# Reordering the first batch of a fused cosine-attention and feed-forward kernel: key tiles ahead of values, transposes ahead of sums

## The chip, the cores and the metric

One core of a Trainium2 chip runs the whole kernel. The metric is device time in microseconds (us): the median over several executions. Beside it stands one profiled execution, from which every duration of an instruction is read. The engines are called by the profile's names: PE (matmul), PEld (its weight loads), DVE (vector), ACT (activation), POOL (general purpose) and SP (issues transfers). Each engine works through its own list of instructions in order and waits at an instruction whose inputs or buffers are not ready.

## The reference

Attention with normalised queries and keys over 8 batches of 12 heads, 448 positions of 64 numbers each, then a feed-forward layer on the 3584 tokens:

```python
def _attn_ref(q, k, v, tau):
    q_n = q / (np.linalg.norm(q, axis=-1, keepdims=True) + 1e-06)
    k_n = k / (np.linalg.norm(k, axis=-1, keepdims=True) + 1e-06)
    scores = np.matmul(q_n, k_n.transpose(0, 1, 3, 2)) / tau
    scores = scores - np.max(scores, axis=-1, keepdims=True)
    attn = np.exp(scores)
    attn = attn / (np.sum(attn, axis=-1, keepdims=True) + 1e-09)
    return np.matmul(attn, v)

def _moe_ref(x, w_in, w_out):          # x: 3584 x 768, w_in: 768 x 2048
    h = x @ w_in
    g = np.maximum(0.01 * h, h)
    return g @ w_out
```

## The kernel before

The unit of attention is a pair of heads (a slot `s`). Batch 0 has six pairs, `s` = 0 to 5; two pairs make a quad `j`. The order of all instructions is written out by hand, and each engine's list is the order of the calls in the Python text.

A pair goes through these steps. `squares(s)` multiplies q and k with themselves on POOL (for pair 0 and half of pair 1 on ACT and DVE). `sums(s, parts)` adds the 64 squares of each row on DVE; part 0 is q, part 1 is k. `roots(s)` makes norms on ACT with two instructions, `Ln` with the tile `tiny` (1e-18) as its bias (L244) and `Exp` with scale 0.5 (L245). `normalise(s)` adds 1e-6, takes reciprocals and writes `qn` (L253, L254, L270, all DVE). `transposes(s)` turns `qn` with seven PE instructions (L284) and copies them from PSUM to `qkT` on DVE (L325). `scores(s, kis)` computes key tiles on PE (L346): tile `ki` is 128 keys against 448 queries for both heads, and an `Exp` on ACT follows it (L355, 128x896). Tile 3 holds the last 64 keys of two pairs, so a quad has seven tiles. `totals(j)` sums the exponentials with 16 PE instructions (L366) and inverts them on ACT with `Ln` and `Exp` (L377, L378). `products(j, e)` are 16 PE instructions each that multiply with the values (also L366), and `scale(j, e)` on DVE (L397) divides them into `xT`, the input of the feed-forward part.

`first(c, m, kts)` are feed-forward products with `w_in` (L494), one PE instruction for each `kt`; six `kt` make an output. `second` multiplies with `w_out` (L527) and copies to `osb` (L538). Output columns `kt` 0 and 1 come from quad 0, 2 and 3 from quad 1, 4 and 5 from quad 2.

PSUM has eight banks. In batch 0 key tiles take turns on two pairs of banks, so the third tile cannot start before the exponential of the first has been read; single banks are the other four. `fill(count)` puts matmuls on PE whose results nobody reads (L603). `WARM` = 22 of them run at the start, before pair 0's data is there. `hold(x)` makes POOL wait for a tile of DVE, so that POOL's squares and transfers keep in step.

The loop over the pairs of batch 0 is this, cut to its PE and ACT steps:

```python
scores(s, (0,))
if s == 1: roots(2)
if j is not None and not even: products(j, 1)
scores(s, (1,)); fill(2)
...            # sums, normalise(s + 1), scale, hold, squares, loads
scores(s, (2,))
if last: first(0, 0..1, (0, 2))
elif not even or s == 0: fill(2)
if n and not even: roots(n)
if not even: scores(s, (3,))
if j is not None and even: totals(j)
if not last: transposes(s + 1)
if j is not None and even: products(j, 0)
if last: first(0, 0..1, (1,))
elif not even or s == 0: fill(2)
if n and even: roots(n)
```

Here `n` = s + 2 for s = 1 to 3, `j` = s // 2 - 1 from s = 2, `even` and `last` speak of `s`. After the loop come `totals(2)`, both `products(2, e)`, then the second batch's pairs (s = 6 to 11) between feed-forward groups, the third part written out with `settle` and `attend(j)` (totals, two products, two scales). From slot 12 on (`OLD`) other functions transpose and multiply in a steady stream (L306, L417, L442) with feed-forward groups between them, to the end.

## Time and profile before

| What | us |
|---|---|
| median of 3 runs | 420.97 (419.59 to 421.17) |
| profiled execution, its own time | 419.61 |
| its span, first to last instruction | 417.8 |
| PE busy | 409.2 (98%) |
| ACT busy | 253.7 (61%) |
| DVE busy | 219.8 (53%) |
| POOL busy | 114.8 (27%) |

The profiled execution's time is its span and 1.8 us around it, and it lies 1.36 us under the median, near the fastest of the runs. PE's busy time counts the `fill` matmuls, 49 in all, as work. Busy shares are averages over stages: batch 0's attention is the first 34 us of the span, and the steady stream begins near 83 us.

### The profile page before, as it was taken

What the parts mean: (1) busy time and instruction counts of PE and PEld (TensorE: products, weight loads), DVE (VectorE), ACT (ScalarE), POOL (GpSimd) and SP (SyncE); (2) the same over time, 40 slices, a digit from 0 to 9 for tenths busy, and PEclk for the clock granted to TensorE, in tenths of its full rate; (3) what the DMA queues carried; (4) which work ended last, traced back from release to release, by engine and by line L of the source; (5) the groups of instructions that cost most, each with busy time, mean ns of one, the idle gap of its engine ahead of it and who ended that gap; (6) DMA issues with size and microseconds to landing.
All of it is one profiled execution on the core that took longest, in us unless ns stands there. A gap on an engine that the chain in (4) does not pass through costs nothing.

```text
span 417.8 us, 11304 instructions
## 1 busy us (share of the span) xinstructions
PE 409.2 (98%) x4793; PEld 212.1 (51%) x4793; DVE 219.8 (53%) x385; ACT 253.7 (61%) x430; POOL 114.8 (27%) x150
## 2 busy tenths in 40 slices
PE   8899999999999999999999999999999999999996
PEld 3334554544455555544455555554445555654563
DVE  6877776866678565765484864464621301210021
ACT  4897877388757786667865688547774464014300
POOL 4877361433234132412331423122210000000000
PEclk9999999999999999999999999999999999999999
DMA  7999998684387941893285681742442100010022
GB/s 187 239 226 213 233 223 172 149 231 115 63 220 191 208 109 33 205 236 91 54 186 154 143 238 48 172 127 83 89 90 77 41 38 3 38 77 0 2 75 75
DMA packets 41810, 53.82 MB, mean 129 GB/s; under 512 B 12448, under 2 KB 32160, under 8 KB 41760
## 3 DMA queue, kind: packets, MB, share of 16 engines
q1 hardware_dynamic: 25584, 40.88, 35.2%
q0 software_dynamic: 15488, 11.80, 19.6%
q8 instruction: 37, 0.61, 0.6%
q10 hardware_dynamic: 688, 0.43, 0.4%
q14 instruction: 13, 0.11, 0.1%
HBM read 45.61 MB, written 11.01 MB: 136 GB/s over the span
## 4 chain that ended last, share of the span: by engine, by line
PE 96%; DVE 2%; ACT 2%; issue 0%; DVEq 0%
PE ps L527 36%; PE ps L494 35%; PE ps L442 9%; PE ps L417 7%; PE ps L366 3%; PE ps L603 3%; PE ps L346 2%; PE ps L284 1%; ACT pe L355 1%; DVE qkT L325 0%; DVE qn L270 0%; DVE ss L231 0%; DVE osb L538 0%; ACT ss L244 0%; ACT norms L245 0%
## 5 line engine op out<-in xcount | busy, mean ns | idle before, releaser
L527 PE MATMUL ps<-w_out_sb,hT 128*128 128x384 bf16 x896 | 151.3, 326 | 0.5 <-DVE xT L397 0.5
L494 PE MATMUL ps<-xT,w_in_sb 128*128 128x384 bf16 (+1 forms) x768 | 151.1, 353 | 0.0
L423 ACT ACTIVATE pe<-ps 128x896 bf16<-128x896 f32 x126 | 108.9, 916 | 44.7 <-PE ps L417 44.7
L527 PEld LDWEIGHTS <-hT 128*128 128x128 bf16 x896 | 85.5, 98 | 65.3 <-issue 10.8
L494 PEld LDWEIGHTS <-w_in_sb 128*128 128x128 bf16 x768 | 72.7, 98 | 74.1 <-issue 9.7
L505 ACT ACTIVATE hT<-ps 128x384 bf16<-128x384 f32 (+1 forms) x128 | 67.3, 553 | 54.7 <-PE ps L494 54.2
L538 DVE COPY osb<-ps 128x384 f32<-128x384 f32 (+1 forms) x56 | 30.9, 551 | 101.3 <-PE ps L527 101.2
L216 POOL TENSOR_TENSOR sq<-qk_h 128x896 f32<-128x896 f32 x36 | 60.4, 1679 | 3.8 <-DMA qk_h<-in_k_dram 3.8
L612 POOL CAST seen<-qn 128x1 f32<-128x1 bf16 x46 | 8.4, 183 | 184.6 <-DVE qn L260 167.8
L260 DVE TENSOR_TENSOR qn<-qk_h,r 128x896 bf16<-128x896 f32 x36 | 42.4, 1179 | 1.2
L355 ACT ACTIVATE pe<-ps 128x896 bf16<-128x896 f32 x42 | 36.0, 919 | 2.9 <-PE ps L346 2.8
L231 DVE TENSOR_REDUCE ss<-sq 128x14 f32<-128x896 f32 x36 | 37.4, 1038 | 0.0
L417 PE MATMUL ps<-qkT 64*32 64x448 bf16 x1008 | 36.5, 353 | 0.0
L253 DVE TENSOR_REDUCE r<-norms 128x14 f32<-128x28 f32 x48 | 8.6, 179 | 51.6 <-ACT norms L245 51.4
L244 ACT ACTIVATE ss<-ss,tiny 128x14 f32<-128x14 f32 x48 | 14.7, 307 | 26.6 <-DVE ss L231 25.7
L467 DVE TENSOR_TENSOR xT<-ps,rb 128x448 bf16<-128x448 f32 x32 | 18.4, 617 | 22.3 <-PE ps L442 21.2
L306 DVE STREAM_TRANSPOSE tt<-qn 128x448 f32<-128x448 f32 x36 | 29.5, 821 | 0.9
L442 PE MATMUL ps<-pe,vq 64*32 64x448 bf16 x1008 | 27.0, 349 | 0.0
L417 PEld LDWEIGHTS <-qkT 64*32 64x32 bf16 x1008 | 13.1, 91 | 19.3 <-issue 14.1
L442 PEld LDWEIGHTS <-vq 64*32 64x32 bf16 x1008 | 14.5, 93 | 8.0 <-issue 0.3
L603 PE MATMUL ps<-pe 128*128 128x512 bf16 x49 | 15.5, 443 | 1.6 <-DVE pe L586 1.6
L346 PE MATMUL ps<-qkT 64*64 64x448 bf16 (+1 forms) x132 | 12.8, 360 | 2.5 <-ACT pe L355 1.6
(55 smaller groups left out, 220.9 us busy)
## 6 DMA issues: line engine op xcount, KB each, us to landing
qk_h<-in_q_dram SPq DMA_DIRECT2D x36, 224.0 KB, 4.4
qk_h<-in_k_dram SPq DMA_DIRECT2D x36, 224.0 KB, 4.4
out_dram<-osb SPq DMA_DIRECT2D x20, 384.0 KB, 3.3
qkT<-tt SPq DMA_DIRECT2D x72, 56.0 KB, 3.1
qkT<-tt SPq DMA_DIRECT2D x36, 112.0 KB, 3.4
vq<-in_v_dram POOLq DMA_DIRECT2D x16, 224.0 KB, 5.0
w_in_sb<-in_moe_w_in_dram POOLq DMA_DIRECT2D x4, 768.0 KB, 11.0
w_out_sb<-in_moe_w_out_dram POOLq DMA_DIRECT2D x2, 1536.0 KB, 21.6
```

Of the source, the lines that this page charges most:

```text
L216: gp.tensor_tensor(sq, raw[s], raw[s], op=ALU.mult)
L231: nc.vector.tensor_reduce(ss[s], sqs[s].rearrange("p (t d) -> p t d", d=D), axis=AX.X, op=ALU.add)
L260: nc.vector.tensor_tensor(qn[s].rearrange("p m d e -> p m e d"), raw[s].rearrange(f"p ({t[1:-1]} d) -> p m e d", e=n, d=D), r.rearrange(f" ...
L306: nc.vector.transpose(out=to.rearrange(("p g (c m) -> p m g c", "p g (m c) -> p m g c")[which], m=7), in_=qn[s].bitcast(F32).rearrange("p ...
L355: nc.scalar.activation(out=dst, in_=sc[:, :, :S], func=AF.Exp, scale=inv_tau)
L417: nc.tensor.matmul(out=sc[32 * strip : 32 * strip + 32, a, :S], lhsT=x[rows, c0 : c0 + 32], rhs=x[rows, 0:S], start=True, stop=True,)
L423: nc.scalar.activation(out=pq[u, i], in_=sc[:, :, :S], func=AF.Exp, scale=inv_tau)
L442: nc.tensor.matmul(out=po[32 * strip : 32 * strip + 32, w, :S], lhsT=weights, rhs=pq[us[x if two else 0], i][rows, a, :], start=(i == 0), ...
L494: nc.tensor.matmul(out=pm[:, :n], lhsT=w_in_sb[:, kt, m * 128 : (m + 1) * 128], rhs=xT[c // 2][:, kt, c0 : c0 + n], start=(done + i == 0), ...
L505: nc.scalar.activation(out=hT[c][:, m, :n], in_=pm[:, :n], func=AF.Prelu, alpha=0.01)
L527: nc.tensor.matmul(out=po2[:, :HALF], lhsT=hT[c][:, m, ts * 128 : (ts + 1) * 128], rhs=w_out_sb[:, m, half * HALF : (half + 1) * HALF], st ...
L538: nc.vector.tensor_copy(out=o[:, half * HALF : half * HALF + cut], in_=po2[:, :cut])
```

## The change

Three things are edited. First, the loop over batch 0's pairs: for s = 3 and s = 5 key tile 1 stands in front of `products(j, 1)`; for s = 1 `roots(3)` moves behind key tile 3; for s = 3 `transposes(4)` moves in front of key tile 3; for s = 4 `transposes(5)` moves in front of `totals(1)` and key tile 0 of pair 5 in front of `products(1, 0)`; for s = 5 the `fill(2)` goes, and the two products `first(0, m, (3,))`, which stood behind `products(2, e)`, join those in front of `totals(2)`.

Second, the 1e-18: the squares of a row are kept in 65 columns, the last set once to 1e-18, so that the sum on DVE adds it and `Ln` has no bias tile. The three tiles of squares, `r` and `seen` become fixed tiles instead of tiles of a pool.

Third, two smaller moves: the first transfer on SP is the 64-row rest of q of pair 0 and no longer its main part, with the two squares and sums of that pair swapped to match; and `roots(s + 6)` (slot 12) stands behind `attend(3)` and not in front of it.

```diff
-            x[:, 0:512].rearrange("p (h t d) -> p h t d", h=2, d=D),
-            x[:, 512:896].rearrange("p (h t d) -> p h t d", h=2, d=D),
+            x[:, 0 : 8 * w].rearrange("p (h t d) -> p h t d", h=2, d=w),
+            x[:, 8 * w : 14 * w].rearrange("p (h t d) -> p h t d", h=2, d=w),
...
-        sq = sqp.tile([128, 14 * D], F32, name="sq")
+        sq = sqt[s % 3]
         if s >= OLD:
             sqs[s] = sq
-            gp.tensor_tensor(sq, raw[s], raw[s], op=ALU.mult)
+            x = raw[s].rearrange("p (t d) -> p t d", d=D)
+            gp.tensor_tensor(sq[:, :, :D], x, x, op=ALU.mult)
...
-                ss[s], sqs[s].rearrange("p (t d) -> p t d", d=D), axis=AX.X, op=ALU.add
+                ss[s], sqs[s], axis=AX.X, op=ALU.add
...
-        nc.scalar.activation(ss[s], ss[s], func=AF.Ln, bias=tiny)
+        nc.scalar.activation(ss[s], ss[s], func=AF.Ln)
...
+    load_rem((0,), (nc.sync, None))
     load_main(0, (nc.sync, nc.scalar))
-    load_rem((0,), (nc.sync, nc.scalar))
+    load_rem((0,), (None, nc.scalar))
...
-    tiny = cpool.tile([128, 1], F32, name="tiny")
-    nc.vector.memset(tiny, 1e-18)
+    sqt = []
+    for i in range(3):
+        sqt.append(cpool.tile([128, 14, D + 1], F32, name=f"sq{i}"))
+        nc.vector.memset(sqt[i][:, :, D], 1e-18)
+    r = cpool.tile([128, 14], F32, name="r")
+    seen = cpool.tile([128, 1], F32, name="seen")
...
-    for t in (slice(0, 3), slice(3, 4)):
+    for t in (slice(3, 4), slice(0, 3)):
...
-        scores(s, (0,))
+        if not last:
+            scores(s, (0,))
         if s == 1:
             roots(2)
+        scores(s, (1,))
         if j is not None and not even:
             products(j, 1)
-        scores(s, (1,))
-        fill(2)
+        if not last:
+            fill(2)
...
         if last:
             for m in range(2):
                 first(0, m, (0, 2))
-        elif not even or s == 0:
+            scores(s, (3,))
+            for kt in (1, 3):
+                for m in range(2):
+                    first(0, m, (kt,))
+        elif not even:
             fill(2)
-        if n and not even:
-            roots(n)
-        if not even:
+            if s == 3:
+                roots(n)
+                transposes(s + 1)
             scores(s, (3,))
-        if j is not None and even:
+            if s == 1:
+                roots(n)
+                transposes(s + 1)
+            fill(2)
+        elif s == 0:
+            fill(2)
+            transposes(1)
+            sums(2)
+            fill(2)
+        else:
+            if s == NPAIR - 2:
+                transposes(s + 1)
             totals(j)
...
+            if s == NPAIR - 2:
+                scores(s + 1, (0,))
+            else:
+                transposes(s + 1)
             products(j, 0)
-        if last:
-            for m in range(2):
-                first(0, m, (1,))
-        elif not even or s == 0:
-            fill(2)
-        if n and even:
-            roots(n)
+            if n:
+                roots(n)
...
-    for m in range(2):
-        first(0, m, (3,))
     for m in range(2, 4):
         first(0, m, range(KT - 2))
...
-    roots(s + 6)
     transposes(s + 5)
     attend(NQ)
+    roots(s + 6)
```

More of the change, by code (lines that the diff above doesn't have):

```diff
@@ L51 @@
     vbp = ctx.enter_context(tc.tile_pool(name="vb", bufs=3))
-    sqp = ctx.enter_context(tc.tile_pool(name="sq", bufs=3))
     smp = ctx.enter_context(tc.tile_pool(name="small", bufs=3))
@@ L118, with halves @@
     OLD = 2 * NEWQ
-    def halves(x):
+    def halves(x, w=D):
         return (
-            x[:, 0:512].rearrange("p (h t d) -> p h t d", h=2, d=D),
-            x[:, 512:896].rearrange("p (h t d) -> p h t d", h=2, d=D),
+            x[:, 0 : 8 * w].rearrange("p (h t d) -> p h t d", h=2, d=w),
+            x[:, 8 * w : 14 * w].rearrange("p (h t d) -> p h t d", h=2, d=w),
         )
@@ L131, in load_rem @@
         for i, (x, eng) in enumerate(zip((q, k), engs)):
+            if eng is None:
+                continue
             eng.dma_start(
@@ L212, in squares @@
             return
-        sq = sqp.tile([128, 14 * D], F32, name="sq")
+        sq = sqt[s % 3]
         if s >= OLD:
             sqs[s] = sq
-            gp.tensor_tensor(sq, raw[s], raw[s], op=ALU.mult)
+            x = raw[s].rearrange("p (t d) -> p t d", d=D)
+            gp.tensor_tensor(sq[:, :, :D], x, x, op=ALU.mult)
             return
-        sqs[s] = halves(sq)
+        sqs[s] = halves(sq.rearrange("p t d -> p (t d)"), D + 1)
         for x, y, eng in zip(raw[s], sqs[s], engs):
             if eng is nc.scalar:
-                nc.scalar.activation(y, x, func=AF.Square)
+                nc.scalar.activation(y[..., :D], x, func=AF.Square)
             else:
-                eng.tensor_tensor(y, x, x, op=ALU.mult)
+                eng.tensor_tensor(y[..., :D], x, x, op=ALU.mult)
     def sums(s, parts=(0, 1)):
@@ L251, in normalise @@
             return
-        r = smp.tile([128, 14], F32, name="r")
         nc.vector.tensor_reduce(r, norms[s % 3], axis=AX.X, op=ALU.add)
@@ L610, in hold @@
     def hold(x):
-        seen = smp.tile([128, 1], F32, name="seen")
         gp.tensor_copy(out=seen, in_=x)
-    sqs[0] = halves(sqp.tile([128, 14 * D], F32, name="sq"))
+    sqs[0] = halves(sqt[0].rearrange("p t d -> p (t d)"), D + 1)
     ss[0] = smp.tile([128, 14], F32, name="ss")
-    nc.vector.tensor_tensor(sqs[0][1], raw[0][1], raw[0][1], op=ALU.mult)
+    nc.vector.tensor_tensor(sqs[0][1][..., :D], raw[0][1], raw[0][1], op=ALU.mult)
     sums(0, (1,))
-    for t in (slice(0, 3), slice(3, 4)):
-        nc.scalar.activation(sqs[0][0][:, :, t], raw[0][0][:, :, t], func=AF.Square)
+    for t in (slice(3, 4), slice(0, 3)):
+        nc.scalar.activation(sqs[0][0][:, :, t, :D], raw[0][0][:, :, t], func=AF.Square)
         nc.vector.tensor_reduce(
@@ L696 @@
                 first(0, m, (0, 2))
-        elif not even or s == 0:
+            scores(s, (3,))
[3 more added lines that the diff above has]
+        elif not even:
             fill(2)
-        if n and not even:
-            roots(n)
-        if not even:
+            if s == 3:
+                roots(n)
+                transposes(s + 1)
             scores(s, (3,))
-        if j is not None and even:
-            totals(j)
-        if not last:
-            transposes(s + 1)
-        if s == 0:
-            sums(2)
-        if j is not None and even:
-            products(j, 0)
-        if last:
-            for m in range(2):
-                first(0, m, (1,))
-        elif not even or s == 0:
-            fill(2)
-        if n and even:
-            roots(n)
+            if s == 1:
[10 more added lines that the diff above has]
+                transposes(s + 1)
+            totals(j)
+            if s == NPAIR - 2:
+                scores(s + 1, (0,))
+            else:
+                transposes(s + 1)
+            products(j, 0)
+            if n:
+                roots(n)
         if j is not None and not even and not last:
```

## The prediction

> **What bounds the kernel now.** I read the page's engine rows first, then PE's waits, then PE and ACT in order of time for the first 66 us, then the chain around the one late wait.

> ```profile
> PE 409.2 (98%) x4793; PEld 212.1 (51%) x4793; DVE 219.8 (53%) x385; ACT 253.7 (61%) x430; POOL 114.8 (27%) x150
> PEclk9999999999999999999999999999999999999999
> ```

> PE is busy for all but 8.6 of 417.8 us, at a full clock. But its busy time holds 49 `fill` matmuls, so where it really could be shorter shows only in its waits:

> ```profile
> PE ps L346 <- ACT pe L355: 1.6, 5, 0.4
> PE ps L603 <- DVE pe L586: 1.6, 1, 1.6
> PE ps L346 <- DVE qkT L325: 0.9, 3, 0.3
> PE ps L527 <- DVE xT L397: 0.5, 1, 0.5
> ```

> The columns are total, times and longest. Apart from the start (1.6 us until the first `fill` has data) there are 3.0 us of waits, and each lies before 64 us: eight at key tiles of batch 0 (L346), one at a feed-forward group (L527). From 64 us on PE waits for nothing, so whatever is won or lost before that is carried to the end unchanged. The windows query says the same of the stretch 9.03 to 34.25: ACT is busy 21.98 of its 25.22 us, the highest share anywhere, and PE runs 28 fill matmuls there. That stretch is paced by ACT and its dependences; behind it PE sets the time. The two kinds of wait in order of time, PE first, then ACT:

> ```profile
> 17.95 0.36 PE L346 MATMUL ps<-qkT 64*128 64x448 bf16 x2 [0.29 <-DVE qkT L325]
> 18.74 0.36 PE L346 MATMUL ps<-qkT 64*128 64x448 bf16 x2 [0.42 <-ACT pe L355]
> ...
> 63.67 2.60 PE L527 MATMUL ps<-w_out_sb,hT 128*128 128x384 bf16 x15 [0.46 <-DVE xT L397]
> ```

> ```profile
> 17.33 0.31 ACT L244 ACTIVATE ss<-ss,tiny 128x14 f32<-128x14 f32 x1 [0.57 <-DVE ss L237]
> ...
> 30.86 0.92 ACT L355 ACTIVATE pe<-ps 128x896 bf16<-128x896 f32 x1 [0.33 <-PE ps L346]
> 32.02 1.75 ACT L355 ACTIVATE pe<-ps 128x896 bf16<-128x896 f32 x2 [0.25 <-PE ps L346]
> ```

> At 17.33 ACT stands in `roots(3)` waiting for a sum, with a finished key tile behind it; at 30.86 and 32.02 it waits for key tiles that PE has put behind products.

> **The change, part by part.**

> *Start, +0.1.* Three memsets of squares columns replace the one of `tiny` ahead of the tile that `fill` reads. The nearest rows are the three `norms` memsets, 0.15 us together, so the first fill starts about 0.1 us later (bounds 0 to 0.2). The 22 warm fills end at 9.03 and pair 0's transposes follow without a wait; `qn` of pair 0 was ready at 8.60. The swap of the two q transfers can bring `qn` forward: the last square waited 1.09 us for the 64-row rest until 5.54, and the main part, now second on SP (0.5 to 0.8 us for an issue), lands at about 4.7. This stays hidden behind the fills; if they ended earlier than 8.6 it would be worth up to 0.4. I take nothing.

> *s = 1, -0.3.* With `roots(3)` behind it, the exponential of key tile (1,3) starts at 16.77, when the one before is through, and not at 17.79. PE then has both banks for pair 2 and the 0.42 wait goes. Next in line is key tile (2,2), which needs the bank of (2,0): that exponential can start at 17.95 + 0.33 = 18.28, ends 0.92 later, so (2,2) starts near 19.24 and not 19.58. That makes 0.34; bounds 0 and 0.42. `roots(3)` ends at about 18.1; `normalise(3)`, which needs it, was at 18.79.

> *s = 3, -0.15.* `transposes(4)` is ahead of key tile 3's four matmuls (0.31), so the copy to `qkT` ends 0.3 earlier and the wait of 0.29 at 26.54 goes. But key tile (4,1) then waits for the exponential of (3,3), which stands behind `roots(5)` on ACT and that behind a sum on DVE, unmoved; about half stays. Bounds 0 and 0.29. The key tile moved ahead of `products(0, 1)` removes 0.25 of ACT's idle time at 23.68 but meets the next `fill`; nothing taken.

> *s = 4 and 5, -0.5.* From the end of key tile (4,2), 28.21, PE now runs transposes 0.50, totals 0.87, three times key tile and products less the last products (0.29 + 0.87 + 0.29 + 0.87 + 0.29), four `first` 0.76, key tile 3 0.31, four `first` 0.76: 5.81, so `totals(2)` starts at 34.02 and not 34.25. Two more of the feed-forward products are then already done (0.19 each), so PE is 0.6 ahead, nearly the 0.54 of the dropped fill. Does ACT keep up? Exponentials now start at 30.44 (when `Exp` of the totals ends), 31.26, 32.24 and 33.32; the last ends at 34.24, before the strips of `totals(2)` that need it (34.60). And `qkT` of pair 5: transposes end at 28.7, the copy takes 0.62, and key tile (5,0) comes at 29.6; covered by 0.25. If that cover were gone the tile would wait as at 26.54, by 0.3. I take 0.5; bounds 0.2 and 0.6. `first` with kt 1 and 3 needs `scale(1, 1)`: the products end at 31.9, a scale is 0.62, use is from 33.3. Its odd weight rows were issued at 19.70 and took 11.3, so they land at 31.0.

> *`Ln` without the bias tile, -0.27.* L244 takes 307 ns, L245, the same shape without a bias tile, 216. I take the difference, 0.09; bounds 0 and 0.09, since both are 128x14 on one engine. Forty-eight such are 4.3 us of ACT, hidden behind PE everywhere but in the first stretch, where `roots(2)`, `(4)` and `(5)` stand in front of exponentials: 3 x 0.09. [...]

> *Squares at a pitch of 65, 0.* No row shows POOL writing rows of 64 at that pitch. The nearest are L216, 1684 ns for a flat 896, and L223, 1040 and 823 ns for 512 and 384 in pieces: 1.00 to 1.11 times the flat one. On DVE, L260 writes 896 interleaved in 1179 ns, as the two contiguous L270 (1160) do. So 0 to 11% on POOL. Between the `hold`s at 12.08, 16.97, 20.56, 24.43 and 28.18 POOL idles 1.50, 0, 1.13 and 0.99, and 0.2 us more for each pair mostly goes into that; cost 0 to 0.2, taken 0. Sums go from 896 to 910 elements, 1038 to about 1054 ns, on a DVE that is half idle. [...]

> *`roots(12)` behind `attend(3)`, -0.46.*

> ```profile
> 60.34 1.00 DVE ss L231
> 61.35 0.02 issue
> 61.37 0.32 ACT ss L244
> 61.69 0.02 issue
> 61.71 0.22 ACT norms L245
> 61.92 0.44 ACT rb L377
> ```

> This chain ends in the 0.46 at 63.67. `totals(3)` ends on PE at 61.0, and L377 could have started then; it stood behind L244, which waited for a sum. Without that it starts at 61.05, the inverse ends at 62.2, the first scale at 62.85, and PE arrives at 63.13: the wait is gone whole. `normalise(12)` needs `roots(12)`, now at 62.7, while DVE is scaling to 63.4; nothing new is late. Bounds 0.2 and 0.46.

> Sum: +0.1 - 0.3 - 0.15 - 0.5 - 0.27 - 0.46 = -1.6. Against the profiled execution (span 417.8, time 419.61) that is a span of 416.2 and 418.0; against the median of the runs, 1.36 above that execution, 419.4. I predict 419.4. The three runs spread over 1.6 us, so the median can sit 0.8 either way. About 0.5%, 2.1 us, is what a measurement of this kernel can tell from no change, and -1.6 is inside it.

> **Rivals.**

> *ACT closes up (faster by more).* Between 10.4 and 34.8 ACT's gaps are 0.85, 0.57, 0.25, 0.27, 0.33, 0.25 and 0.16: 2.7 us. If the reordering lets key tiles run ahead everywhere, those go, with five `Ln` (0.45) and the 0.46: -3.6, 417.4. From -2.1 on it counts as faster. For it: ACT is the busiest there, and every move puts key tiles earlier. Against: the gap of 0.85 belongs to pair 0, whose order is not touched, and pairs 2 to 4 still wait for their own norms. Chance 0.28.

> *The gain is given back to transfers.* DMA's busy share is 1.15 from 9 to 34 us and 1.27 to 64, so landings do not move with PE. Values of quad 2 were issued at 22.48 and took 10.9, landing at 33.4, used at 34.3 after the change; `w_out`'s first half 30.95 + 23.3 = 54.3, used at 55.9; values of quad 3 at 57.6, used at 59.8. The margins are 0.9 to 2.2 us, not much for a stretch with a full DMA. Landings a microsecond or two later give all but 0.5 back: 420.5. Chance 0.15.

> *POOL becomes the pace (slower).* If writing at a pitch of 65 doubles POOL's multiply, 1.82 us are added for each of four pairs, 7.3, less the 3.6 of idle time above: 3.7 lost, and every later pair of batch 0 waits in its sums. With -1.6 that is +2.1, 423.1; from there on it is slower by over 0.5%, so from a factor of about 2. For it: one sum (0.29 at 18.18) already waits for POOL. Against: no row comes near a factor of 2. Chance 0.07.

> **How the numbers follow.** The forecast has 0.50; of it 0.04 falls past 2.1 us. Faster: 0.28 + 0.04 = 0.32. Slower: 0.07 and 0.01 from the transfers, 0.08. Same: 0.60. The range goes from 417.5, the end of the first rival, to 421.2, the second with a run's spread, and leaves out the third and some noise, under 2 in 10.

> **What would show it.** After the change: L346's waits for ACT and DVE fall from 2.5 to about 1.4 us, L527's wait is gone, L244 takes about 215 ns, L603 counts 47, and `totals(2)` starts near 33.4 with eight feed-forward products before it. It is wrong if L223 or L216 grow beyond 10%, if PE shows a wait for a DMA, if the wait at the end of `attend(3)` is still there, or if ACT's gaps before 35 us sum to under 1 us.

## The result and the profile after

The changed kernel takes 419.31 us (median of 22 runs, 418.14 to 420.99), the kernel before 420.00 in the 22 runs beside them. The ratio is 0.9978 with an interval of 0.9969 to 0.9987: faster by about 0.9 us, within the 0.5% called no change. The forecast time of 419.4 was met, in part by luck: it starts from 420.97, the median of three runs, and the 22 runs put the kernel before at 420.00. From there the forecast gain of 1.6 us leads to 418.4; the gain by the medians is 0.7, so it was forecast too large by 0.9, and the two errors cancel.

The profiled execution of the changed kernel is the slowest of its 22: span 419.2, 1.4 longer than the one before. That makes it a good one for seeing what takes the gain back. Its engine row and PE's waits (line, releaser, total us, times, longest):

```profile
PE 409.2 (98%) x4791; PEld 211.6 (50%) x4791; DVE 222.1 (53%) x387; ACT 249.8 (60%) x430; POOL 114.7 (27%) x150
```

```profile
PE ps L367 <- DMA v_b<-in_v_dram: 1.3, 1, 1.3
PE ps L347 <- ACT pe L356: 1.3, 5, 0.3
PE ps L528 <- DMA w_out_sb<-in_moe_w_out_dram: 0.6, 1, 0.6
PE ps L285 <- DVE qn L271: 0.5, 1, 0.5
PE ps L347 <- DVE qkT L326: 0.3, 1, 0.3
PE ps L347 <- ACT norms L247: 0.3, 1, 0.3
```

(All lines after the first edit have moved by one to six.) The key tiles' waits fell from 2.5 to 1.9 us, less far than the 1.4 forecast, and the late wait for a scale is gone, as forecast. Three waits are new: for the values of quad 2, for the first half of `w_out`, and for a `qn`. Together they are 2.4 us. A wait of PE for a DMA was one of the signs by which the prediction said that it would be wrong, and two of the three are such waits. In order of time on PE:

```profile
18.22 0.55 PE L347 MATMUL ps<-qkT 64*128 64x448 bf16 x4 [0.29 <-ACT norms L247]
...
33.60 0.75 PE L367 MATMUL ps<-pe,ones 128*32 128x448 bf16 x12
34.18 0.36 PE L367 MATMUL ps<-pe,ones_rem 128*32 128x448 bf16 x4
35.85 0.75 PE L367 MATMUL ps<-pe,v_b 128*32 128x448 bf16 x12 [1.31 <-DMA v_b<-in_v_dram]
...
58.09 2.77 PE L528 MATMUL ps<-w_out_sb,hT 128*128 128x384 bf16 x16 [0.61 <-DMA w_out_sb<-in_moe_w_out_dram]
```

At 18.22 both key tiles of pair 2 now run as one group of four matmuls: the 0.42 between them is gone. `totals(2)` starts at 33.60 and not at 34.25, with eight feed-forward products before it in place of six. Two rows later PE stands 1.31 us for values. On ACT the four exponentials of pair 5 are now one row without a gap, where there were gaps of 0.33, 0.25 and 0.16:

```profile
30.33 3.56 ACT L356 ACTIVATE pe<-ps 128x896 bf16<-128x896 f32 x4
```

The operations whose price was in doubt, from the costliest groups:

```profile
L246 ACT ACTIVATE ss<-ss 128x14 f32<-128x14 f32 x48 | 10.3, 215 | 23.8 <-DVE ss L233 23.1
L218 POOL TENSOR_TENSOR sq<-qk_h 128x896 f32<-128x896 f32 x36 | 60.5, 1681 | 3.6 <-DMA qk_h<-in_k_dram 3.5
L233 DVE TENSOR_REDUCE ss<-sq 128x14 f32<-128x910 f32 x36 | 37.8, 1051 | 0.0
```

`Ln` without the bias tile takes 215 ns, 92 less than the 307 before. POOL writes at the pitch of 65 in 1681 ns, against 1679 flat, before: of the 0 to 11% that the prediction left open nothing shows.

### The profile page after: what moved, and what is told of

Read it like the earlier page. It is cut to its first block, busy times and chain, and to the rows that moved or that the text cites. A ratio compares the mean times of both kernels' runs of the same rounds, so it can differ in the third digit from the quotient of the medians.

```text
span 419.2 us, 11314 instructions
## 1 busy us (share of the span) xinstructions
PE 409.2 (98%) x4791; PEld 211.6 (50%) x4791; DVE 222.1 (53%) x387; ACT 249.8 (60%) x430; POOL 114.7 (27%) x150
## 4 chain that ended last, share of the span: by engine, by line
PE 89%; DMA 5%; SPq 2%; POOL 1%; DVE 1%; issue 0%; ACT 0%; DVEq 0%; POOLq 0%
PE ps L495 35%; PE ps L528 35%; PE ps L443 9%; PE ps L418 7%; DMA v_b<-in_v_dram 3%; PE ps L367 2%; DMA xT<-in_q_dram 1%; PE ps L347 1%; DMA qk_h<-in_q_dram 1%; POOL sq L225 1%; DVE qn L271 1%; PE ps L285 1%; SPq L141 0%; SPq L133 0%; SPq L142 0%; SPq L163 0%
## 5 line engine op out<-in xcount | busy, mean ns | idle before, releaser
L528 PE MATMUL ps<-w_out_sb,hT 128*128 128x384 bf16 x896 | 151.3, 326 | 0.6 <-DMA w_out_sb<-in_moe_w_out_dram 0.6
L528 PEld LDWEIGHTS <-hT 128*128 128x128 bf16 x896 | 85.4, 98 | 65.5 <-issue 10.0
L506 ACT ACTIVATE hT<-ps 128x384 bf16<-128x384 f32 (+1 forms) x128 | 67.5, 553 | 57.6 <-PE ps L495 56.4
L218 POOL TENSOR_TENSOR sq<-qk_h 128x896 f32<-128x896 f32 x36 | 60.5, 1681 | 3.6 <-DMA qk_h<-in_k_dram 3.5
L233 DVE TENSOR_REDUCE ss<-sq 128x14 f32<-128x910 f32 x36 | 37.8, 1051 | 0.0
L418 PE MATMUL ps<-qkT 64*32 64x448 bf16 x1008 | 36.7, 353 | 0.0
L307 DVE STREAM_TRANSPOSE tt<-qn 128x448 f32<-128x448 f32 x36 | 29.6, 822 | 0.9
L246 ACT ACTIVATE ss<-ss 128x14 f32<-128x14 f32 x48 | 10.3, 215 | 23.8 <-DVE ss L233 23.1
L418 PEld LDWEIGHTS <-qkT 64*32 64x32 bf16 x1008 | 13.2, 91 | 19.3 <-issue 14.1
L443 PE MATMUL ps<-pe,ones 64*32 64x448 bf16 x560 | 15.1, 349 | 0.0
```

The costliest lines, as they stand in the source:

```text
L218: gp.tensor_tensor(sq[:, :, :D], x, x, op=ALU.mult)
L233: nc.vector.tensor_reduce(ss[s], sqs[s], axis=AX.X, op=ALU.add)
L307: nc.vector.transpose(out=to.rearrange(("p g (c m) -> p m g c", "p g (m c) -> p m g c")[which], m=7), in_=qn[s].bitcast(F32).rearrange("p ...
L418: nc.tensor.matmul(out=sc[32 * strip : 32 * strip + 32, a, :S], lhsT=x[rows, c0 : c0 + 32], rhs=x[rows, 0:S], start=True, stop=True,)
L443: nc.tensor.matmul(out=po[32 * strip : 32 * strip + 32, w, :S], lhsT=weights, rhs=pq[us[x if two else 0], i][rows, a, :], start=(i == 0), ...
L506: nc.scalar.activation(out=hT[c][:, m, :n], in_=pm[:, :n], func=AF.Prelu, alpha=0.01)
```

## The experiments

Theory A: the reordering wins what was worked out, and landings of transfers give a part back, a different part in each execution. Against it stood B, the reordering or the start being worth less by itself, and later C, that the reordered kernels bring the landings later.

### The changed kernel again

No edit.

> The changed kernel once more, for a second profiled execution and for what it stands to the kernel before. Theory A (the reorder wins about 1.4 us on PE before 34 us, and landings of the values of quad 2 and of the first half of w_out give a varying part back): PE's order up to totals(2) is as in the first trace, 1.3 to 1.5 us ahead net of the start; the waits of L367 for v_b (1.31 us in the first trace) and of L528 for w_out (0.61) come out differently, together between 0 and 2 us, and the span is lower by as much as they are shorter. Rival B (the start is what gives back: fills end 0.35 us later and the rest is small): the waits for transfers are the same or absent and the start is again 0.3 to 0.4 us later. Ratio about 0.998 under both.

Measured: 418.91 us, ratio 0.9972 (0.9961 to 0.9983), span of the profiled execution 417.1. PE's waits of that trace:

```profile
PE ps L347 <- ACT pe L356: 1.3, 5, 0.3
PE ps L528 <- DMA w_out_sb<-in_moe_w_out_dram: 1.2, 1, 1.2
PE ps L347 <- DVE qkT L649: 0.3, 1, 0.3
```

The wait for values is absent, that for `w_out` twice as long. The two traces of one kernel differ by 2.1 us in span and by nothing in the order: from the first key tile to `totals(2)` both take exactly 23.24 us (24.25 before), so in that stretch what PE and ACT do is the same to 0.01 us. The waits for transfers are 0.7 us less in this trace. The expectation let the span fall by no more than that; the first key tile also comes 0.41 us earlier (9.95 for 10.36, the warm fills taking 6.96 for 7.74), and the wait of 0.51 for `qn` is gone. B, a start that is late again, is not what this trace shows: the first key tile was at 10.00 in the kernel before.

### One part of the change alone

Three runs put one part each into the kernel before; the swap of pair 0's transfers has its run further down.

```diff
 # only the loop over batch 0's pairs, with first(0, m, (3,)) in it
 # only the column of 1e-18, Ln without bias, the fixed tiles
 # only this move
-    roots(s + 6)
     transposes(s + 5)
     attend(NQ)
+    roots(s + 6)
```

> The kernel before with the loop over batch 0's pairs alone reordered (key tiles, transposes, the ten feed-forward products, the dropped fill). Prediction's terms for it: -0.3 - 0.15 - 0.5 = -0.95 us, less what landings take. Theory A: about 1 us ahead at totals(2), a wait for v_b of 0 to 1 us, ratio 0.9975 to 0.9995. Rival B: a ratio of 0.9977, the full -0.95, since the start is that of before.

> The kernel before with the column of 1e-18 and the fixed tiles alone: Ln without a bias tile, squares at a pitch of 65, three memsets more. Prediction's terms: +0.1 - 0.27 = -0.17 us, and nothing for POOL, so a ratio of 0.9996 (0.999 to 1.000). L246-type Ln near 215 ns, POOL's squares 1040 and 823 ns as before. Rival B, if the start is later by 0.35 us through the memsets: ratio 1.000 to 1.001.

> The kernel before with roots(12) behind attend(3) alone. Prediction's term: -0.46 us, ratio 0.9989; the wait of L527 for DVE's scale at 63.67 is gone. If landings are already what PE meets at 57 to 64 us in the kernel before, less: ratio 1.000.

| Part alone | forecast, us | ratio | interval | us of 420 |
|---|---|---|---|---|
| loop | -0.95 | 1.0000 | 0.9987 to 1.0012 | 0.0 |
| column | -0.17 | 0.9989 | 0.9980 to 0.9998 | -0.5 |
| `roots(12)` | -0.46 | 0.9987 | 0.9979 to 0.9996 | -0.55 |

The three sum to -1.0, near the whole change's -0.9 (its second measurement gives -1.2); each interval is some 0.5 us either way, so the agreement is no proof that the parts add up. `roots(12)` does what was worked out: no wait at the second feed-forward group is left in its trace. The loop, the largest term, gives nothing: A had expected 0.9975 to 0.9995, and the measured 1.0000 lies just above that, while B's full 0.9977 lies outside the interval. Its trace says where it went:

```profile
PE ps L527 <- DMA w_out_sb<-in_moe_w_out_dram: 0.9, 1, 0.9
PE ps L366 <- DMA v_b<-in_v_dram: 0.7, 1, 0.7
PE ps L346 <- DVE qkT L325: 0.6, 2, 0.3
PE ps L494 <- DMA w_in_sb<-in_moe_w_in_dram: 0.5, 1, 0.5
```

From the first key tile to `totals(2)` it takes 23.99, of which 0.46 is the wait for `w_in`: without that 23.53, 0.72 less than before, and two more products of 0.19 are done, so the order wins 1.1. In this execution PE stands 2.0 us in all for three transfers and the span is 419.3. That an average over executions comes to zero fits this; the traces of one execution each don't prove it. The column's trace is 0.19 us shorter over the same stretch (forecast 0.27 of `Ln`); the other 0.3 of its ratio the trace does not show, and the interval allows it to be noise.

### The kernel before again

No edit.

> The kernel before, unchanged, for a second profiled execution. Its first trace has the first half of w_out landing at 54.2 and no wait for a transfer; traces of the kernels run since have it at 54.2 to 58.2. Theory A (landings vary from execution to execution by up to 4 us, whatever the kernel): it lands somewhere between 54 and 58, and PE waits for it if it is later than 57.0. Rival C (the reordered kernels bring the landing later by themselves, through other transfers being issued earlier): it lands at 54 to 55 again and PE waits for no transfer.

Measured: ratio 1.0003 (0.9990 to 1.0016), span 418.4. `w_out`'s first half lands at 56.4 and not at 54.2, in the same kernel, and PE reaches it at about 57.2. So landings move by 2 us between executions of one kernel, as A has it. PE itself waits for none of them. The range of A was 54 to 58, that of C 54 to 55; but C is not gone. Landings of that half, as issue plus time to landing from the rows of its line:

| Kernel | issued | took | landed |
|---|---|---|---|
| before, two traces | 30.95, 31.20 | 23.3, 25.2 | 54.2, 56.4 |
| only `roots(12)` | 31.02 | 24.7 | 55.7 |
| only column | 30.64 | 27.0 | 57.6 |
| only loop | 30.39 | 27.8 | 58.2 |
| changed, two traces | 30.38, 29.97 | 27.7, 26.8 | 58.1, 56.8 |
| changed, 20 fills | 30.68 | 27.4 | 58.1 |
| changed, no swap | 30.43 | 25.9 | 56.3 |

With the loop reordered it takes 25.9 to 27.8, without it 23.3 to 27.0. One trace for each is too little to say that the order itself slows the transfers. What is shown: PE comes to its first use at 57.0 to 57.2 in the kernel before and at 55.6 to 57.5 in the changed one (start of the group less its wait), and the landings lie across it.

### Transfers issued earlier

Four runs issue transfers of the first stretch one pair earlier on POOL: the changed kernel with all of them (the diff) and with the values alone, the kernel before with all, and the loop alone with all.

```diff
-        if s in (1, 2):
-            load_v(s)
+        if s == 1:
+            load_v(2)
...
-        elif s < 2:
+        elif s < 4:
             load_w_in(s)
-        elif s > 2:
-            load_w_in(s - 1)
+        else:
+            load_w_out(0)
+        if s == 0:
+            load_v(1)
```

> The changed kernel with the values of quads 1 and 2, the last two quarters of w_in and the first half of w_out each issued one pair earlier on POOL, in places where POOL has idle time or where another transfer stood; nothing else moves. Theory A: L367 and L528 no longer wait for a transfer, each execution is near the fastest of the changed kernel, 418.2 to 418.6 us, ratio to before 0.995 to 0.997. Rival B: no change against the changed kernel, ratio 0.998. If DMA as a whole is what is late (its busy share is above 1 there), the wait moves to another tile, w_in or q and k, and the ratio stays at 0.998 or is worse.

> The changed kernel with only the values of quads 1 and 2 issued one pair earlier, w_in and w_out where they were. Theory A: the wait of L367 for v_b is gone, that of L528 for w_out stays or grows by as much as PE is earlier there (up to 1 us). Ratio 0.996 to 0.998, above the run with all transfers earlier if w_out is the second limit.

> The kernel before with the transfers issued one pair earlier as in the run of the changed kernel with that edit. Theory A: the kernel before comes later to the values of quad 2 and to w_out and waits for neither, so nothing is won, ratio 0.9995 to 1.001. If it is faster by 1 us or more, landings held back the kernel before as well, and the earlier transfers are a gain of their own.

> The kernel before with the reordered loop and the transfers issued one pair earlier. The loop alone gave a ratio of 1.000, the earlier transfers alone 1.0006. Theory A (the loop's gain was lost to landings): together 0.9975 to 0.9985, PE waits for no transfer. Rival B (the reordering is worth nothing by itself): 1.000.

| Kernel with earlier transfers | ratio | interval | longest wait for a transfer in its trace |
|---|---|---|---|
| changed, all | 0.9979 | 0.9968 to 0.9990 | none |
| changed, values only | 0.9984 | 0.9967 to 1.0001 | `w_in` 2.7 |
| before, all | 1.0006 | 0.9997 to 1.0016 | none |
| loop alone, all | 1.0010 | 0.9991 to 1.0030 | `w_in` 1.4 |

```profile
PE ps L495 <- DMA w_in_sb<-in_moe_w_in_dram: 2.7, 1, 2.7
```

That is the run with the values alone: they land at 30.6, and the second quarter of `w_in`, issued behind them, lands at 35.9 where it landed at 31.4 and 32.5 in the changed kernel. Behind the earlier transfer the later one landed 3.4 to 4.5 us later here: the wait moved to another tile, the third of the outcomes that the expectation named. In all five traces with the values issued first that quarter takes 13.0 to 15.6 us to land, against 11.3 to 13.5 in the nine others. What A forecast for all transfers earlier, 0.995 to 0.997, was missed; for the values alone A had named a wait for `w_out`, and it came at `w_in`. Only the kernel before came out as A had it, with nothing won. In the one trace of the changed kernel with all transfers earlier and no wait for any, the stretch from the first key tile to the steady stream at L418 takes 71.94 us, against 73.04 before: 1.1 less. The traces with the old issue order say the same by subtraction. In the four of the changed loop (the two of the changed kernel, 20 fills, no swap) this stretch takes 72.25 to 73.97; less each trace's waits for transfers, and for the `qn` behind them, it is 71.2 to 71.7, 1.4 to 1.9 less than the 73.04. That is the 1.7 that the terms behind the start add up to. So the traces carry A; the times do not decide, because as a whole the kernel with earlier transfers is no faster than without. The loop with earlier transfers was to tell A from B by the time, and didn't: its ratio is that of B, its trace shows the wait of 1.4 that A is about.

### The start

Two runs on the first 10 us: 20 warm fills for 22, and the swap of pair 0's transfers undone.

```diff
-    WARM = 22
+    WARM = 20
```

```diff
-    load_rem((0,), (nc.sync, None))
     load_main(0, (nc.sync, nc.scalar))
-    load_rem((0,), (None, nc.scalar))
+    load_rem((0,), (nc.sync, nc.scalar))
...
-    for t in (slice(3, 4), slice(0, 3)):
+    for t in (slice(0, 3), slice(3, 4)):
```

> The changed kernel with 20 warm fills and not 22. In its trace qn of pair 0 is ready at 8.59 and the fills end near 9.4; two fewer take 0.43 us at the full clock. If the fills set the start: first key tile 0.4 us earlier, and the end 0.4 us earlier where no transfer is late, 0 where one is. Theory A: ratio against before 0.997 to 0.998. If qn is the later one: no change, 0.998.

> The changed kernel with the swap of pair 0's first transfers and squares undone. In the traces with the swap roots(0) starts at 6.41, 6.44, 7.11 and 7.34, in the one with the column and without the swap at 6.12. If the swap delays the start: roots(0) at 6.1, first key tile at 9.8 to 10.1 unless the fills end later, a ratio 0.001 to 0.002 below the changed kernel's 0.9975, so 0.9955 to 0.9965; less where w_out lands late, since what is won at the start is waited for at 57 us. If the swap is neutral: 0.9975.

Measured: 20 fills 0.9995 (0.9984 to 1.0005), no swap 0.9983 (0.9970 to 0.9995). The first misses the expected 0.997 to 0.998; the second misses 0.9955 to 0.9965, expected if the swap delays the start, and agrees with the 0.9975 of a swap that is neutral. In the trace with 20 fills PE waits 0.55 for pair 0's `qn`, so fewer fills could win nothing there. The two squares of q on ACT, in the kernel before and then in that trace:

```profile
3.93 0.52 ACT L621 ACTIVATE sq<-xT 128x384 f32<-128x384 f32 x1 [1.91 <-DMA xT<-in_q_dram]
5.54 0.31 ACT L621 ACTIVATE sq<-xT 128x128 f32<-128x128 f32 x1 [1.09 <-DMA xT<-in_q_dram]
...
5.29 0.31 ACT L626 ACTIVATE sq<-xT 128x128 f32<-128x128 f32 x1 [3.27 <-DMA xT<-in_k_dram]
5.96 0.52 ACT L626 ACTIVATE sq<-xT 128x384 f32<-128x384 f32 x1 [0.36 <-DMA xT<-in_q_dram]
7.11 0.21 ACT L246 ACTIVATE ss<-ss 128x14 f32<-128x14 f32 x1 [0.63 <-DVE ss L627]
```

The small square stands first now, but its 128 partitions are 64 rows of q and 64 of k, and k's part is still second on ACT's own queue, so it waits for that until 5.29. The long square then waits for its own data: q's main part, issued at 1.58 and no longer at 0.74, takes 4.4 us and lands at 5.9. The prediction had it at 4.7; in the five traces with the swap the long square starts at 5.26 to 6.19, each time behind a wait for this transfer. The longer sum is now the last, and `roots(0)` starts at 6.41 to 7.34 in these five and at 6.12 to 6.36 in the nine without.

Whether PE feels it depends on the execution. In the changed kernel's own two traces `qn` of pair 0 is ready at 8.59 and 8.56, as early as before (8.60), and PE does not wait for it. The first key tile is 0.36 late in the first of them because the first fill starts 0.05 later and the 22 fills take 0.31 longer; in the second it comes 0.05 earlier than before. In the other three with the swap `qn` is ready at 9.26 to 9.48 and PE waits 0.55 to 0.89 for it. Without the swap it is ready at 8.54 to 9.02, and in three traces of nine PE waits 0.41 to 0.54. The first key tile comes at 10.50 in the mean with the swap (9.95 to 10.88) and at 10.14 without (9.93 to 10.41). So no gain of the swap shows, and it can cost; 0.36 is a difference of means with the fills' own spread in it. The run without it shows no gain either: in its trace the first key tile comes at 10.41, and PE waits 0.4 for `w_out`.

### Both: no swap, transfers earlier

> The changed kernel with the swap undone and the transfers issued one pair earlier: what the experiments point to. Theory A with a swap that costs: no wait for a transfer before 64 us, start as before, all terms of the prediction stand, -1.6 us, ratio 0.9955 to 0.9965, and the lowest of all. If landings are bound by DMA as a whole: no better than without earlier transfers, 0.9965 to 0.9975.

Measured: 421.02 us, ratio 1.0013 (0.9992 to 1.0035), runs from 418.94 to 423.67; the trace has a wait of 2.4 us for `w_in`, landing at 35.2. Both expectations are missed. Part of the loss is not the wait itself: the granted clock of PE reads about 0.5 around its end, and the work behind it takes 1.30 us longer (last section). So this is no better version, and none of the variants is clearly under the changed kernel.

## Why the prediction was right and where it was wrong

**Right: the steps on PE and ACT.** The terms of the first stretch without the start were -0.3 - 0.15 - 0.5 - 0.27 = -1.22. Measured from the first key tile to `totals(2)`: 24.25 to 23.24, and two more products of 0.19 done, -1.39. It is the same in four traces of the changed order (23.24 or 23.25). Step by step it also fits: up to key tile (2,2) -0.35, from there to (4,2) -0.45, from there to `totals(2)` -0.21 and the two products' -0.38. The terms with 0.09 for each of the three `Ln` were -0.39, -0.33 and -0.5. `Ln` fell by the 92 ns taken from the row beside it. The wait of 0.46 went, and the part alone gave -0.55.

**Wrong: the margin of transfers.** The prediction listed margins of 0.9 to 2.2 us from one trace, took them for sure in the forecast and gave the case that they fail 0.15. It is the ordinary case: all four traces of the changed loop with the other parts and the old issue order have a wait for a transfer. The values of quad 2 took 10.9 in the trace that was read and 11.1 to 13.1 in the other traces with the old issue order; `w_out`'s half took 23.3 and then 24.7 to 27.8. That trace was the luckiest of all. With the wait for `qn` that can follow, 0.9 to 2.4 us are given back in these four. "Landings a microsecond or two later give all but 0.5 back" was the right mechanism; the step that failed is its chance. How much an average execution gives back no trace shows: the kernel before loses something too in some of its own (its second trace takes 0.39 us longer over the same stretch), and what is left of the gain is 0.7 by the medians and 0.9 by the ratio.

**Wrong: the swap at the start.** It was costed at nothing with a gain of up to 0.4 left open, on a landing at 4.7 for q's main part. By the rows that part landed no earlier than 5.2 in any of the five traces, and the small square had to wait for k's part, which the prediction did not look at. No gain shows; the cost lies between nothing and some 0.9 us in an execution, and its average is not shown. The +0.1 of the memsets was 0.05: the first fill starts at 1.65 for 1.60.

**Right: POOL.** The rival on its pace is refuted by 1681 ns. The first rival did not come: ACT's gaps in the first stretch fell from 2.7 only to 2.2 us, with the 0.85 at pair 0 still there and a new one of 0.44 at 18.63. (One count of the prediction is off without consequence: the timeline has 27 fill matmuls between the warm ones and `totals(2)`, the 49 less 22, and not 28.)

**Not settled:** how the gain left over divides between a smaller win and what landings take, whether the new order itself makes `w_out` land later, and why the column alone is worth 0.5 where its trace shows 0.2.

## What to carry to other kernels

A gain on the engine that paces a stretch can be taken back by the next thing that lands: here 1.39 us were won on PE up to `totals(2)`, and 0.9 to 2.4 given back in four traces. Before summing terms, take landing times from several executions, not from one, since the compute order repeated to 0.01 us here while the landing of `w_out` moved by 2 us within one kernel. Issuing the values earlier made a quarter of `w_in` later (35.9 for 31.4 and 32.5); whether fewer bytes or a later use would help was not tried. When a transfer is brought forward on its queue, price the one that now goes behind it, and look for the operation's other input. And take the median that a forecast starts from over many runs: three were 1 us off.

## What the runs showed of the hardware that was not expected

**PE's clock read about 0.5 around the end of the two longest waits.** In the run with the values alone, PE stands 2.73 us for `w_in`, and the page's row of granted clock shows a dip in its fourth slice; the same four products behind a wait of 1.39, in the loop with earlier transfers, take their usual time:

```profile
PEclk9998999999999999999999999999999999999999
35.94 1.46 PE L495 MATMUL ps<-xT,w_in_sb 128*128 128x384 bf16 x4 [2.73 <-DMA w_in_sb<-in_moe_w_in_dram]
...
34.33 0.82 PE L494 MATMUL ps<-xT,w_in_sb 128*128 128x384 bf16 x4 [1.39 <-DMA w_in_sb<-in_moe_w_in_dram]
```

**Two multiplies on DVE took 3.36 us beside one on POOL.** In the trace of the changed kernel POOL's transfer waited for the landing of `w_out`, and its squares then met `normalise(11)`; both engines in order of time:

```profile
58.19 3.36 DVE L271 TENSOR_TENSOR qn<-qk_h,r 128x512 bf16<-128x512 f32 x2
58.58 0.82 POOL L178 DMA_DIRECT2D v_b<-in_v_dram  x1 [2.20 <-DMA w_out_sb<-in_moe_w_out_dram]
59.42 1.69 POOL L218 TENSOR_TENSOR sq<-qk_h 128x896 f32<-128x896 f32 x1
61.67 0.18 POOL L617 CAST seen<-qn 128x1 f32<-128x1 bf16 x1 [0.56 <-DVE qn L271]
61.81 1.68 POOL L218 TENSOR_TENSOR sq<-qk_h 128x896 f32<-128x896 f32 x1
61.93 1.09 DVE L233 TENSOR_REDUCE ss<-sq 128x14 f32<-128x910 f32 x1
```

The two DVE multiplies take 3.36 us, against 1.16 in the second trace, where they ended before POOL began. The sum at 61.93 beside the next squares takes 1.09, near the 1.05 that the 36 sums of this form take in the mean. So a late landing can cost twice: here PE's wait of 0.61, and 0.51 for `qn`. It needs no late landing, though: in the kernel before the two multiplies meet POOL's squares as well and take 1.67 us in its first trace and 2.42 in its second. The multiply was stretched and the sum was not; why, no trace shows.

**The warm fills differ from execution to execution.** The 22 of them take between 6.32 and 7.74 us in the 13 traces that have them. At first one takes 0.63 us and the next starts 0.43 after it, later one takes 0.38 and the next starts 0.21 to 0.22 after it; in the loop with earlier transfers the faster pace is there from about 4.6 us on, in the changed kernel's first trace from 7.5. The profile's granted clock reads 1.00 all the while and does not show this. So where the fills end moves by 1.4 us, and with it whether fills or `qn` of pair 0 set the start.
